# Weight subtractions moved on GpSimd and VectorE, and the gates computed ahead of the fill matmuls, in a Fourier mix followed by a mixture of experts

## The chip, the core and the metric

The kernel runs on one core of a Trainium2 chip. The core has TensorE (PE in the rows; PEld is its weight load), VectorE (DVE), ScalarE (ACT), GpSimd (POOL) and SyncE (SP, which here only issues DMAs). The metric is the time on the device in microseconds. Before the change the median of three runs was 593.81 us (592.75 to 595.03).

## The reference

The input x has 8 batches of 2496 tokens with 256 features. A Fourier transform along the tokens, a complex 256x256 product, a soft threshold and the inverse transform give 19968 rows; then each row is sent to one of 8 experts, and each expert computes only the 80 rows with the largest gate.

```python
X = np.fft.rfft(x, axis=1)
Yr = Xr @ w_r - Xi @ w_i + b_r
Yi = Xr @ w_i + Xi @ w_r + b_i
Yr = np.sign(Yr) * np.maximum(np.abs(Yr) - lam, 0.0)      # Yi too
y = np.fft.irfft(Yr + 1j * Yi, n=2496, axis=1)
...
logits = x @ w_gate                                      # x is y as (19968, 256)
expert_idx = np.argmax(logits, axis=1)
probs = softmax(logits); gate_w = probs[arange(N), expert_idx]
for e in range(8):
    tok_idx = the capacity=80 rows of expert e with the largest gate_w
    h = np.maximum(x[tok_idx] @ w1[e], 0.0)
    out[tok_idx] = gate_w[tok_idx, None] * (h @ w2[e])
```

## The kernel before

Both transforms are products with small tables, cut into stages: stageA and stageB are the forward transform (39 x 64 points), stageC the complex product with the soft threshold, stageT a transform over three classes on DVE, stageD a transposition back with the gate columns beside it, stageHB the last inverse step whose result goes to DRAM (`hd`). A loop over 16 steps (8 batches, two halves each) runs these stages interleaved. Values are split into a 16-bit high part and the remainder, so most products are three matmuls. Beside this, the 8 experts' weights are loaded in pieces of 128x1024, and each piece is split the same way: ACT copies the high part (L837, L840, L843) and a subtraction writes the low part, on POOL (L849) or, for the five pieces in the list `WV`, on DVE (L846). The pieces of experts 0 to 5 and part of 7 go to POOL; DVE has the four pieces of expert 6, numbered (k, i) with k = 0 for the first matrix and k = 1 for the second, and one of expert 7.

The last step of the loop (`if end`, L1500) is the second half of batch 7. Its stageC results (L441 matmuls, L450 on ACT, L456 and L458 on DVE) go to stageG1 (L676 matmuls), which computes the gate scores of this half directly. stageG0 and stageE1c complete the scores, `back` (L750) transposes them, stageE2 (L758 to L780) makes softmax gates, level1 and the rounds of level2 (L946 to L952) find each expert's best, and `pick` merges two lists (L1020 to L1027) and writes `posA`, the rows to gather (L1271). The function `stageT` (L503 to L508) and its copies (L516, L517) of the half before run on DVE at the beginning of this last step; `junk` (L1516) is a copy of one element on POOL that waits for them and that holds what is behind it on POOL.

From `posA` on POOL issues indirect DMAs: `tok` (row numbers), `hx` (the pieces of a row, two gathers for each group of 128 rows) and `wv` (their coefficients); `position` sums the pieces, `columnsY` transposes the sums into `xT`, `ffn1` (L1230, L1232, L1234) and `ffn2` (L1246, L1247) are the two products of an expert, and `give` scatters the rows into the output. `busy` (L1195) issues matmuls whose result is not used, to keep TensorE's clock up while the gathers run: 16 in front of the gate matmuls, 22 behind them. `rows` (L1274, L1276) turns the chosen gates into a column for each gathered row, with the help of `flat` (L1002, L1007), which spreads the 8 lists over a diagonal by multiplying with an identity and sums over TensorE. `flags` (L1034 to L1043) checks whether the quick selection may have missed a row.

The order of the instructions on each engine is set by a scheduler that goes by its own estimate of times. Three things steer it: `tc.high_priority()`, `tc.issue_after(i)` (not ahead of instruction i; `behind` is the same with a name), and `pin`, which keeps the written order.

## Time and profile before

| | before |
|---|---|
| median of 3 runs | 593.81 us |
| profiled execution, its own time | 594.43 us |
| its span | 592.6 us |
| PE busy | 531.8 us (90%) |
| DVE busy | 393.4 us (66%) |
| POOL busy | 379.3 us (64%) |
| ACT busy | 324.8 us (55%) |

The span is the time between the first and the last instruction of the profiled execution; what lies around it is 594.43 - 592.6 = 1.8 us. A row of a timeline has the start in us from the span's beginning, the time that the instructions take together, the engine, the line of the kernel, the operation, what is written and read with its size, and how many there are; in square brackets is how long the engine stood idle before it, and what it then waited for.

### The profile page before, as it was taken

To read this page: it belongs to the slowest core of one execution; us is meant where nothing else is said; L and a number is where in the kernel's file an instruction comes from. 1 tells how busy PE (TensorE), PEld (TensorE's weight loads), DVE (VectorE), ACT (ScalarE), POOL (GpSimd) and SP (SyncE) were. 2 spreads that over 40 slices of the span, in tenths; PEclk is the share of its full clock that TensorE was granted. 3 is DMA by queue.
4 is the path that set the end of the run, shared out by engine and by line. 5 is a ranking of instruction groups with operands and counts; after the bars stand their busy time and mean duration, and the time that the engine had idled before them with its cause. 6 is when DMAs were issued, how large, how long until landed. Compare 5 with 4: busy or idle time off the path is not lost.

```text
span 592.6 us, 12886 instructions
## 1 busy us (share of the span) xinstructions
PE 531.8 (90%) x5037; PEld 387.8 (65%) x5037; DVE 393.4 (66%) x738; ACT 324.8 (55%) x466; POOL 379.3 (64%) x301
## 2 busy tenths in 40 slices
PE   7869999999999999999999999896999598879683
PEld 2356576668677776877686777665767485448583
DVE  4423555666766667666777866768999847957550
ACT  2324868575756756575666566655646325623461
POOL 4104887686857777786778675688843634867571
PEclk9969999999999999999999999998999757996898
DMA  6887898987989789888979887999827766568810
GB/s 205 263 234 212 306 213 278 268 277 227 270 254 316 196 248 279 263 242 254 289 221 263 249 244 175 309 270 282 237 69 207 198 212 196 134 223 293 292 56 24
DMA packets 97225, 137.02 MB, mean 231 GB/s; under 512 B 26601, under 2 KB 77809, under 8 KB 95403
## 3 DMA queue, kind: packets, MB, share of 16 engines
q1 hardware_dynamic: 91115, 118.10, 69.3%
q0 software_dynamic: 2624, 11.45, 5.5%
q10 hardware_dynamic: 3418, 6.58, 3.4%
q8 instruction: 41, 0.67, 0.5%
q14 instruction: 27, 0.21, 0.1%
HBM read 70.82 MB, written 65.29 MB: 230 GB/s over the span
## 4 chain that ended last, share of the span: by engine, by line
PE 39%; DVE 14%; issue 14%; POOL 14%; DMA 12%; ACT 5%; SPq 1%; POOLq 0%; ACTq 0%; DVEq 0%
PE ps L441 20%; PE ps L311 5%; POOL pair L849 4%; PE ps L607 4%; DMA wt<-in_moe_w 4%; DVE R L470 2%; DMA xt<-in_x 2%; DMA hx<-hd,tok 2%; POOL R L473 2%; ACT tp L465 2%; PE ps L382 1%; PE ps L544 1%; PE ps L383 1%; PE ps L384 1%; PE ps L545 1%
## 5 line engine op out<-in xcount | busy, mean ns | idle before, releaser
L441 PE MATMUL ps<-XT,WM 128*128 128x288 f16 (+4 forms) x1536 | 217.0, 298 | 9.3 <-DVE R L470 3.8
L441 PEld LDWEIGHTS <-WM 128*128 128x128 f16 x1536 | 149.2, 98 | 66.9 <-issue 9.1
L470 DVE SCALAR_TENSOR_TENSOR R<-ps,thr,tp 128x674 f32<-128x674 f32 (+1 forms) x56 | 48.6, 867 | 76.4 <-ACT tp L465 72.7
L488 POOL TENSOR_TENSOR YT<-R,YT 128x1408 f16<-128x1408 f32 (+1 forms) x28 | 73.5, 2624 | 31.9 <-ACT YT L487 28.5
L465 ACT ACTIVATE tp<-ps,thr 128x674 f32<-128x674 f32 (+1 forms) x56 | 43.5, 777 | 79.1 <-PE ps L441 77.2
L473 POOL TENSOR_TENSOR R<-R,sgs 128x576 f32<-128x576 f32 x28 | 36.5, 1302 | 74.3 <-DVE R L470 74.3
L297 POOL TENSOR_TENSOR xs<-xt,xs 117x1024 f16<-117x1024 f32 (+1 forms) x39 | 76.2, 1956 | 9.9 <-ACT xs L296 9.8
L382 PE MATMUL ps<-t2s,z 128*128 128x128 f16 x320 | 59.3, 225 | 9.0 <-DMA z<-zs 7.7
L388 DVE TENSOR_TENSOR XT<-ps,XT 128x640 f16<-128x640 f32 (+2 forms) x64 | 51.7, 814 | 18.9 <-ACT XT L387 18.3
L333 DVE TENSOR_TENSOR zs<-ps,zs 128x1024 f16<-128x1024 f32 (+1 forms) x45 | 51.1, 1135 | 18.7 <-ACT zs L332 18.4
L383 PE MATMUL ps<-t2s,z 128*128 128x128 f16 x320 | 59.2, 224 | 0.0
L384 PE MATMUL ps<-t2s,z 128*128 128x128 f16 x320 | 59.2, 224 | 0.0
L387 ACT ACTIVATE XT<-ps 128x640 f16<-128x640 f32 (+2 forms) x64 | 44.4, 700 | 25.1 <-PE ps L384 22.7
L311 PE MATMUL ps<-xs,t1s 117*128 117x512 f16 x213 | 52.5, 379 | 1.0 <-POOL xs L297 0.8
L607 PE MATMUL ps<-YO,vqs 128*128 128x512 f16 (+1 forms) x252 | 48.6, 333 | 1.9 <-DVE hs L614 1.9
L332 ACT ACTIVATE zs<-ps 128x1024 f16<-128x1024 f32 (+1 forms) x45 | 42.9, 954 | 12.5 <-PE ps L311 6.3
L556 DVE TENSOR_TENSOR YO<-ps,YO 128x768 f16<-128x768 f32 (+1 forms) x50 | 45.3, 906 | 6.0 <-ACT YO L555 6.0
L487 ACT ACTIVATE YT<-R 128x1408 f16<-128x1408 f32 (+1 forms) x28 | 35.5, 1267 | 20.7 <-POOL R L484 20.7
L544 PE MATMUL ps<-wgi,YT 128*128 128x144 f16 (+1 forms) x302 | 43.9, 231 | 1.6 <-DVE R L470 1.3
L545 PE MATMUL ps<-wgi,YT 128*128 128x136 f16 (+1 forms) x302 | 43.2, 227 | 0.0
L555 ACT ACTIVATE YO<-ps 128x768 f16<-128x768 f32 (+1 forms) x50 | 38.5, 776 | 3.1 <-PE ps L545 1.4
L607 PEld LDWEIGHTS <-vqs 128*128 128x128 f16 x252 | 24.5, 99 | 23.8 <-issue 3.3
(317 smaller groups left out, 997.1 us busy)
## 6 DMA issues: line engine op xcount, KB each, us to landing
out<-zero SPq DMA_DIRECT2D x48, 384.0 KB
hd<-hs SPq DMA_DIRECT2D x94, 192.0 KB
z<-zs SPq DMA_DIRECT2D x35, 512.0 KB
xt<-in_x SPq DMA_DIRECT2D x41, 312.0 KB
z<-z SPq DMA_DIRECT2D x14, 528.0 KB
z<-z SPq DMA_DIRECT2D x14, 432.0 KB
wt<-in_moe_w ACTq DMA_DIRECT2D x10, 512.0 KB
pair<-in_moe_w SPq DMA_DIRECT2D x10, 512.0 KB
```

Source lines behind the costliest of these rows:

```text
L297: nc.gpsimd.tensor_tensor(xs[:, 1, :ng], xt[:, j0:j0 + ng], xs[:, 0, :ng], op=ALU.subtract)
L311: nc.tensor.matmul(pt[:, 512 * j:512 * j + 512], t1s[:, t], xs[:, h, 2 * j:2 * j + 2], start=(i == 0), stop=(i == 2))
L333: evD.append(nc.vector.tensor_tensor(zs[:, :ng, 1, :], pv[:, :ng], zs[:, :ng, 0, :], op=ALU.subtract))
L382: nc.tensor.matmul(o, zz(0), t2s[:, cl, 0, :], start=True, stop=False)
L383: nc.tensor.matmul(o, zz(0), t2s[:, cl, 1, :], start=False, stop=False)
L384: nc.tensor.matmul(o, zz(1), t2s[:, cl, 0, :], start=False, stop=True)
L388: nc.vector.tensor_tensor(ov(1), pv, ov(0), op=ALU.subtract)
L441: nc.tensor.matmul(pt[:, o:o + e - a], WM[:, dh, m, wh, 128 * eh:128 * eh + 128], XT[:, dh, xh, c, a:e], start=(i == 0), stop=(i == len(te ...
L465: acts.append(nc.scalar.activation(fv(t), pv, AF.Relu, bias=thr[:, eh, ri, 0:1]))
L470: nc.vector.scalar_tensor_tensor(fv(Rf), pv, thr[:, eh, ri, 1:2], fv(t), op0=ALU.add, op1=ALU.min)
L488: nc.gpsimd.tensor_tensor(yv(1), rv, yv(0), op=ALU.subtract)
L607: nc.tensor.matmul(o, tab[:, v], yo(h), start=(i == 0), stop=(i == 2))
```

## The change

Six edits. In the last step's first block, two subtractions (expert 3's first matrix) are held back in a list, and `junk` is issued first; they and the next two (expert 2's second matrix) are issued behind it. The last two copies and subtractions of that block are issued behind stageD's copy (`dev`) and not behind `acts`. The comparison L1021 goes from `merge` into `flags`. `rows` and `flags` are called in `pick`, with 6 fill matmuls ahead of them, and their small tiles lie in pools that are open by then; the later fill is 32. `flat` can take the identity from PSUM, into which it is copied first. The DVE subtractions of expert 6's second matrix (k = 1) are held back in `dheld` and issued in `experts`, behind `rv` of expert 0 (L1234).

```diff
--- before.py
+++ after.py
...
@@ -799,6 +801,7 @@
     dev, late, dvs = [], [], []
     LW = 7
     wdma = nc.scalar.dma_start
+    hold, held = [], []
     WV = [(6, 0, 0), (6, 0, 1)] + [(6, 1, 0), (6, 1, 1)] + [(7, 1, 1)]
 
     def prepW(e, pool, name):
@@ -842,11 +845,18 @@
                 with tc.issue_after((exps[-2], exps[-2], d2s[0], exps[-1])[2 * k + i].ins) if after else ExitStack():
                     nc.scalar.activation(wh[:, c:c + 1024], wt, AF.Copy)
             if (e, k, i) in WV:
-                with behind(("A", 'xv', (3, 4)[k])) if e == 7 and after else tc.issue_after((ffs if after and e == 6 and k + i else sels)[-1].ins):
-                    nc.vector.tensor_tensor(wl[:, c:c + 1024], wt, wh[:, c:c + 1024], op=ALU.subtract)
+                sub = lambda: nc.vector.tensor_tensor(wl[:, c:c + 1024], wt, wh[:, c:c + 1024], op=ALU.subtract)
+                if e == 6 and k and after:
+                    dheld.append(sub)
+                else:
+                    with behind(("A", 'xv', (3, 4)[k])) if e == 7 and after else tc.issue_after((ffs if after else sels)[-1].ins):
+                        sub()
             else:
-              with tc.issue_after(sums[-1].ins) if sums and e > 4 else ExitStack():
-                nc.gpsimd.tensor_tensor(wl[:, c:c + 1024], wt, wh[:, c:c + 1024], op=ALU.subtract)
+
+                def sub():
+                    with tc.issue_after(sums[-1].ins) if sums and e > 4 else ExitStack():
+                        nc.gpsimd.tensor_tensor(wl[:, c:c + 1024], wt, wh[:, c:c + 1024], op=ALU.subtract)
+                held.append(sub) if hold else sub()
         return [(e, lambda k=k, i=i: step(k, i), lambda k=k, i=i: load(k, i)) for k in range(2) for i in range(2)]
 
     def weight(e, k):
@@ -995,13 +1005,17 @@
 
     hevs = []
 
-    def flat(v, n, dt, late=None, px=None):
+    def flat(v, n, dt, late=None, px=None, eye=None):
 
         px = (sp.tile([8, 8 * CAP], dt, name="pxw") if px is None else px)[:, :8 * n].rearrange("p (e r) -> p e r", e=8)
+        pt = psum()
         with tc.issue_after(late[-1].ins) if late else ExitStack():
-            nc.vector.tensor_tensor(px, v.unsqueeze(1).to_broadcast([8, 8, n]), (eye8 if dt == F16 else ident)[:8, :8].unsqueeze(2).to_broadcast([8, 8, n]), op=ALU.mult)
+            i8 = (eye8 if dt == F16 else ident)[:8, :8]
+            if eye:
+                nc.vector.tensor_copy(pt[:8, 512:520], i8)
+                i8 = pt[:8, 512:520]
+            nc.vector.tensor_tensor(px, v.unsqueeze(1).to_broadcast([8, 8, n]), i8.unsqueeze(2).to_broadcast([8, 8, n]), op=ALU.mult)
         px = px.rearrange("p e r -> p (e r)")
-        pt = psum()
         m = n // 16
         for g in range(m):
             flats.append(nc.tensor.matmul(pt[:, g:g + 1], px[:, 128 * g:128 * g + 128], ones8h if dt == F16 else ones8, start=True, stop=True))
@@ -1018,7 +1032,6 @@
         fl = const.tile([128, 2, 8], F32, name="fl", tag="tk1")[:8, 0, :2]
         g, dp = room[:, :NEW], room[:, NEW:2 * NEW]
         nc.vector.tensor_scalar(fl[:, 0:1], v[:, k:k + 1], GATE_MIN, None, op0=ALU.max)
-        nc.vector.tensor_tensor(fl[:, 0:1], nv[:, NEW - 1:NEW], fl[:, 0:1], op=ALU.is_ge)
         rv, rp = nv[:, ::-1], np_[:, ::-1]
         nc.vector.tensor_tensor(g, rv, v[:, k:], op=ALU.is_gt)
         nc.vector.tensor_tensor(dp, rp, p[:, k:], op=ALU.subtract)
@@ -1029,18 +1042,20 @@
 
     def flags(bg, nw, fl):
         v, m, nm = bg[0], bg[2], nw[2]
-        th = sp.tile([8, 1], F32, name="th")
+        th = const.tile([128, 2, 8], F32, name="th", tag="tk3")[:8, 0, 0:1]
         with tc.issue_after(sels[-1].ins):
             nc.vector.tensor_reduce(out=th, in_=v, op=ALU.min, axis=AX.X)
         nc.vector.tensor_scalar(th, th, GATE_MIN, None, op0=ALU.max)
         with tc.issue_after(sels[-1].ins):
             nc.vector.tensor_tensor(m, m, nm, op=ALU.max)
+            nc.vector.tensor_tensor(fl[:, 0:1], nw[0][:, NEW - 1:NEW], fl[:, 0:1], op=ALU.is_ge)
         nc.vector.tensor_tensor(fl[:, 1:2], m, th, op=ALU.is_ge)
         pt = psum()
         fls.append(nc.tensor.matmul(pt[0:1, 0:2], ones8, fl, start=True, stop=True))
-        ff = sp.tile([1, 1], F32, name="ff")
+        ff = const.tile([128, 2, 8], F32, name="ff", tag="tk4")[:1, 0, 0:1]
         nc.vector.tensor_reduce(out=ff, in_=pt[0:1, 0:2], op=ALU.add, axis=AX.X)
-        ffs.append(nc.vector.tensor_copy(flag, ff))
+        with tc.issue_after(idms[-1].ins):
+            ffs.append(nc.vector.tensor_copy(flag, ff))
 
     NG = E * CAP // 128
 
@@ -1195,7 +1210,7 @@
             warms.append(nc.tensor.matmul(pt, w[:, 0:128], w[:, 0:512], start=True, stop=True))
 
     warms = []
-    BUSY = (16, 22)
+    BUSY = (6, 32)
 
     def columnsY(nm, g, y, xT, pt):
         if isinstance(y, tuple):
@@ -1271,8 +1286,9 @@
         sels.append(nc.vector.tensor_tensor(posA, pr, dl, op=ALU.add))
 
     def rows(nm, v, S):
-        nc.vector.tensor_scalar(gateA, flat(v, CAP, F32, sels), 1.0 / XS, None, op0=ALU.mult)
-        idm = sp.tile([128, NG], F32, name="idm" + nm)
+        A = nm == "A"
+        nc.vector.tensor_scalar(gateA, flat(v, CAP, F32, sels if A else None, px=spare()[:8] if A else None, eye=A), 1.0 / XS, None, op0=ALU.mult)
+        idm = const.tile([128, 2, 8], F32, name="idm", tag="tk5")[:, 0, :NG]
         idms.append(nc.vector.tensor_scalar(idm, gateA, GATE_MIN / XS, BIG, op0=ALU.is_lt, op1=ALU.mult))
 
         def rest():
@@ -1342,6 +1358,9 @@
         feedY(S)
         feedY(S)
         first(0)
+        with behind((S["nm"], "rv", 0)):
+            while dheld:
+                dheld.pop(0)()
         for e in range(E):
             h = hps.pop(e)
             if e:
@@ -1501,8 +1520,10 @@
             doC(0, 0)
             for k in range(4):
                 wq[k][2]()
+            hold.append(1)
             with tc.issue_after(acts[-1].ins):
                 doW(2)
+            hold.clear()
             with tc.issue_after(hbs[-1].ins):
                 while zq:
                     zfill()
@@ -1513,15 +1534,19 @@
             stageG1(b, RR[0], 0)
             with tc.high_priority():
                 stageG1(b, RR[1], 1)
-            pin(nc.gpsimd.tensor_copy(junk, prev[2][0:1, 1, 1, 0, 0, 0:1]))
-            with tc.issue_after(mids[-1].ins):
-                doW(2)
-            with tc.issue_after(acts[-1].ins):
-                doW(2)
+            jk = nc.gpsimd.tensor_copy(junk, prev[2][0:1, 1, 1, 0, 0, 0:1])
+            pin(jk)
+            with tc.issue_after(jk.ins):
+                while held:
+                    held.pop(0)()
+                with tc.issue_after(mids[-1].ins):
+                    doW(2)
             with tc.issue_after(cops[-1].ins):
                 doD()
             with tc.high_priority():
                 back = stageE1c(b, stageG0(b, prev[2]))
+            with tc.issue_after(dev[-1].ins):
+                doW(2)
             p = pend.pop()
             sc6 = stageE2(*p)
             doHB()
@@ -1671,11 +1696,16 @@
         pb_ = places("b", bg[1], CAP, 0.0)
         fl = merge((bg[0], pb_, bg[2]), (nw[0], places("n", nw[1], NEW, 512.0), nw[2]))
         choose(bg[0], pb_)
-        return fl
+        pt = psum()
+        for _ in range(BUSY[0]):
+            nc.tensor.matmul(pt[:, 0:512], pairs[0, 0][0][:, 0:128], pairs[0, 0][0][:, 0:512], start=True, stop=True)
+        rows("A", bg[0], S0)
+        flags(bg, nw, fl)
 
     with tc.issue_after(hops[-1].ins):
         doHB()
-    fl = pick()
+    S0 = {}
+    pick()
     flush()
     stacks[0].close()
     eks.close()
@@ -1697,11 +1727,9 @@
         pct = ctx.enter_context(tc.tile_pool(name="pct", bufs=1, space=PSUM, reuse_waits="tile"))
         pyp = ctx.enter_context(tc.tile_pool(name="pyp", bufs=1, space=PSUM, reuse_waits="tile"))
         pf = ctx.enter_context(tc.tile_pool(name="pf", bufs=4, space=PSUM, reuse_waits="tile"))
-        busy(BUSY[0], pairs[0, 0][0])
         sA = begin("A", NG, posA, cid[0:R2])
-        with tc.issue_after(warms[-1].ins):
-            rows("A", bg[0], sA)
-        flags(bg, nw, fl)
+        S0.update(ct=sA["ct"])
+        sA.update(rest=S0["rest"])
     doW(len(wq) - 4)
     with tc.issue_after(fls[-1].ins), tc.high_priority():
         busy(BUSY[1], pairs[0, 0][0])
```

The list `gps` is only written. The rows below are the engines' instruction orders; line numbers are those of the version that they belong to.

On POOL, in the last step of the loop, before the change (L458 and L517 belong to the stages, L849 is a weight subtraction, `pair_6064` holds expert 3, `pair2b` expert 2's second matrix):

```order
L458 TENSOR_TENSOR R<-R,sgs 128x9x64
L517 TENSOR_TENSOR YT_5755<-R,YT_5755 128x1408
L849 TENSOR_TENSOR pair_6064<-wt,pair_6064 128x1024 x2
L849 TENSOR_TENSOR pair2b<-st,pair2b 128x1024 x2
L1516 COPY junk<-YT_5755 1x1
L849 TENSOR_TENSOR pair_6064<-wt,pair_6064 128x1024 x2
```

and after it (L460, L519, L858 and L1537 are the same instructions' new lines):

```order
L460 TENSOR_TENSOR R<-R,sgs 128x9x64
L519 TENSOR_TENSOR YT_5755<-R,YT_5755 128x1408
L1537 COPY junk<-YT_5755 1x1
L858 TENSOR_TENSOR pair_6064<-wt,pair_6064 128x1024 x2
L858 TENSOR_TENSOR pair2b<-st,pair2b 128x1024 x2
L858 TENSOR_TENSOR pair_6064<-wt,pair_6064 128x1024 x2
```

Four subtractions stood ahead of the copy; all six now stand behind it.

On ACT a little later, before (L843 are weight copies, L666 and L555 belong to stageG0 and stageD, L771 is the exponential of batch 6):

```order
L450 ACTIVATE tp_144<-ps,thr 128x576
L843 ACTIVATE pair_6064<-wt 128x1024 x2
L666 ACTIVATE gp<-ps 128x88
L555 ACTIVATE YO_6071<-ps 128x2x256
L771 ACTIVATE gex<-ps 78x256
```

and after (L452, L846, L668, L557 and L773):

```order
L452 ACTIVATE tp_144<-ps,thr 128x576
L668 ACTIVATE gp<-ps 128x88
L557 ACTIVATE YO_6071<-ps 128x2x256
L846 ACTIVATE pair_6064<-wt 128x1024 x2
L773 ACTIVATE gex<-ps 78x256
```

The two copies went from ahead of stageG0's copy to directly ahead of the exponential.

On DVE behind `posA`, before (L846 are subtractions of expert 6, L1145 is the first work on gathered rows):

```order
L1271 TENSOR_TENSOR posA<-ps,dl 128x5
L1037 TENSOR_TENSOR t2b<-t2b,gh 8x1
L846 TENSOR_TENSOR pair_6811<-pair_6451,pair_6811 128x1024
L1002 TENSOR_TENSOR pxw<-t0b,ident 8x640
L1034 TENSOR_REDUCE th<-t0b 8x1
...
L1043 CAST flag<-ff 1x1
L846 TENSOR_TENSOR pair_6811<-pair_6451,pair_6811 128x1024 x3
L1145 TENSOR_TENSOR wt<-ident,wv 128x128
```

and after (L1015 is the copy of the identity, L1051 the moved comparison, L848 the subtractions):

```order
L1286 TENSOR_TENSOR posA<-ps,dl 128x5
L1015 COPY ps<-ident 8x8
L1047 TENSOR_REDUCE th<-t0b 8x1
L1050 TENSOR_TENSOR t2b<-t2b,gh 8x1
L1051 TENSOR_TENSOR fl<-gh,fl 8x1
L1017 TENSOR_TENSOR Gs<-t0b,ps 8x640
...
L1058 CAST flag<-ff 1x1
L848 TENSOR_TENSOR pair_6802<-pair_6451,pair_6802 128x1024 x2
L1160 TENSOR_TENSOR wt<-ident,wv 128x128
```

One subtraction left the place between `posA` and the gates, one left the place behind the flag; both now stand behind the second `L1249` (L1234 before) of expert 0, ahead of `xT` of group 1.

## Rows read from the trace of the kernel before

**Rows 1.** The page, part 1: an engine's busy time, share and instructions.

```profile
PE 531.8 (90%) x5037; PEld 387.8 (65%) x5037; DVE 393.4 (66%) x738; ACT 324.8 (55%) x466; POOL 379.3 (64%) x301
```

**Rows 2.** Windows: length; PE, PEld, DVE, ACT, POOL busy; granted clock, DMA share, GB/s.

```profile
466.00:468.00 2.00, 0.00 (x0) 0.00 (x0) 1.08 (x4) 1.33 (x2) 0.23 (x1) 0.88 0.06 19
...
486.00:488.00 2.00, 2.00 (x11) 0.99 (x9) 2.00 (x8) 0.43 (x1) 2.00 (x2) 0.50 0.04 8
```

**Rows 3.** Timeline of PE.

```profile
455.65 8.99 PE L441 MATMUL ps<-XT,WM 128*128 128x320 f16 x72
471.97 7.88 PE L676 MATMUL ps<-wgm,R 128*128 128x40 f32 x36 [7.33 <-DVE R L458]
...
532.65 1.22 PE L1209 MATMUL ps<-wt,hx 128*128 128x128 f32 x4 [2.81 <-DVE wt L1145]
```

**Rows 4.** Timeline of POOL in the last step.

```profile
456.64 4.79 POOL L849 TENSOR_TENSOR pair<-wt,pair 128x1024 bf16<-128x1024 f32 x2 [4.13 <-ACT pair L843]
461.40 4.83 POOL L849 TENSOR_TENSOR pair2b<-st,pair2b 128x1024 bf16<-128x1024 f32 x2
...
485.56 4.21 POOL L849 TENSOR_TENSOR pair<-pair,pair 128x1024 bf16<-128x1024 f32 x2 [9.05 <-PE ps L736]
```

**Rows 5.** Tile hs from 440 us: smallest, median, largest ns, first and last start.

```profile
L505 DVE TENSOR_TENSOR R<-R,hs x2: 548/1462/2375, 445.0 to 457.1; 128x384 f32<-128x384 f32 x2
L506 DVE SCALAR_TENSOR_TENSOR R<-hs,R x2: 559/1155/1751, 445.6 to 460.1; 128x384 f32<-128x384 f32 x2
L507 DVE SCALAR_TENSOR_TENSOR R<-hs,R x2: 558/1460/2362, 446.2 to 461.9; 128x384 f32<-128x384 f32 x2
L508 DVE SCALAR_TENSOR_TENSOR R<-hs,R x2: 548/1454/2360, 447.6 to 464.3; 128x384 f32<-128x384 f32 x2
```

**Rows 6.** Timeline of DVE in the last step.

```profile
457.07 2.38 DVE L505 TENSOR_TENSOR R<-R,hs 128x384 f32<-128x384 f32 x1
459.37 0.80 DVE L456 SCALAR_TENSOR_TENSOR R<-ps,thr,tp 128x576 f32<-128x576 f32 x1
...
468.08 1.62 DVE L517 TENSOR_TENSOR YT<-R,YT 128x1408 f16<-128x1408 f32 x1 [0.97 <-ACT YT L516]
```

**Rows 7.** Timeline of ACT in the last step.

```profile
466.67 1.38 ACT L516 ACTIVATE YT<-R 128x1408 f16<-128x1408 f32 x1 [7.11 <-DVE R L508]
...
473.14 1.06 ACT L843 ACTIVATE pair<-wt 128x1024 f16<-128x1024 f32 x1 [0.92 <-DMA wt<-in_moe_w]
...
481.91 0.60 ACT L555 ACTIVATE YO<-ps 128x512 f16<-128x512 f32 x1
484.16 0.38 ACT L771 ACTIVATE gex<-ps 78x256 f32<-78x256 f32 x1 [1.65 <-DVE ps L770]
```

**Rows 8.** Timeline of SP's queue: the second weight load into the staging halves.

```profile
468.71 0.67 SPq L822 DMA_DIRECT2D wt<-in_moe_w  x1
```

**Rows 9.** Timeline of DVE and of POOL at the end of the selection.

```profile
515.27 1.04 DVE L1021 TENSOR_TENSOR fl<-gh,fl 8x1 f32<-8x1 f32 x1
...
512.08 4.23 POOL L849 TENSOR_TENSOR pair<-pair,pair 128x1024 bf16<-128x1024 f32 x2
```

**Rows 10.** Timeline of POOL and of DVE behind posA.

```profile
519.81 1.84 POOL L1094 DMA_INDIRECT tok<-cid,posA  x1 [3.50 <-DMA hd<-hs]
521.96 0.96 POOL L1094 DMA_INDIRECT tok<-cid,posA  x1 [0.31 <-issue]
525.74 1.88 POOL L1094 DMA_INDIRECT hx<-hd,tok  x1 [2.83 <-issue]
...
519.50 1.21 DVE L846 TENSOR_TENSOR pair<-pair,pair 128x1024 bf16<-128x1024 f32 x1
...
524.45 3.50 DVE L846 TENSOR_TENSOR pair<-pair,pair 128x1024 bf16<-128x1024 f32 x3
```

**Rows 11.** Timeline of DVE, and the chain that ended last (start, us, what).

```profile
545.04 0.42 DVE L1217 TENSOR_TENSOR xT<-ps,xT 128x256 f16<-128x256 f32 x1 [1.52 <-ACT xT L1216]
...
547.75 8.17 DMA hx<-hd,tok
```

More of the change, by code (lines that the diff above doesn't have):

```diff
@@ L415, in fourier_mix_then_moe @@
     mids = []
+    gps = []
+    dheld = []
     d2s = []
@@ L645, in stageE1a @@
         gp = ek.tile([128, 2, 20, 8], F16, name="gp", bufs=2)
-        nc.scalar.activation(gp[:, 0], G, AF.Copy)
+        gps.append(nc.scalar.activation(gp[:, 0], G, AF.Copy))
         nc.vector.tensor_tensor(gp[:, 1], G, gp[:, 0], op=ALU.subtract)
@@ L665, in stageG0 @@
         nc.vector.tensor_reduce(out=G, in_=pt[:, 0:176].rearrange("p (c h e) -> p c e h", h=2, e=8), op=ALU.add, axis=AX.X)
-        nc.scalar.activation(gp[:, 0], G, AF.Copy)
+        gps.append(nc.scalar.activation(gp[:, 0], G, AF.Copy))
         nc.vector.tensor_tensor(gp[:, 1], G, gp[:, 0], op=ALU.subtract)
```

## Prediction

> **What bounds the kernel now.** I read the page first: no engine is full over the whole span (PE 90%), so the time has to be read by stretches [rows 1]. A table of 2 us windows then shows where PE stands still near the end: from 466 to 468 PE does nothing, its clock falls there, and it is still at half speed (0.50, the 1.2 GHz level) at 486 [rows 2]. From there on the kernel is a chain of short steps (gate scores of the last batch, selection, gathers, experts) in which every delay is passed on to the end.
>
> The timelines of the three engines say why PE stood still. PE ends its last L441 matmul at 455.65 + 8.99 = 464.64 and begins L676 (stageG1) at 471.97, waiting 7.33 us for DVE's L458 [rows 3]. DVE was late because POOL ran four weight subtractions (L849) from 456.64 to 466.23 [rows 4]. Inside that time DVE's L505 to L508 took 2.375, 1.751, 2.362 and 2.360 us, where the same four took 0.548, 0.559, 0.558 and 0.548 us ten microseconds earlier: the smallest and the largest of each line's two instances stand in its row [rows 5]. All four read two operands from SBUF. L456 at 459.37, which reads PSUM and one SBUF tile, took 0.80 us in the same stretch [rows 6]. So a DVE instruction with two SBUF inputs lasts until POOL's running instruction ends, and one with a PSUM input does not care.
>
> **The change part by part, against the profiled execution (594.43 us with a span of 592.6; the median of the three runs shown is 593.81, 0.6 lower).**
>
> 1. *The subtractions go behind the junk copy.* Four of POOL's six subtractions of this stretch now stand behind the one-element copy that waits for DVE's L517; the other two stood there already. While L505 to L508 run, POOL is idle. They give back 8.85 - 2.21 = 6.6 us. I walk it through: DVE 457.07 + 0.55 + 0.80 + 0.56 + 0.56 + 0.55 = 460.1; ACT's L516 (1.38) to 461.5; L517 (1.62) to 463.1, where it ended at 469.70 [rows 6, 7]. From there to L676 nothing is changed: 471.97 - 6.6 = 465.4. PE's last L441 ends at 464.64, before that, so PE does not bind first. Value -6.6; the bounds are -7.3 (the whole gap on PE) and -4 (one blocked instruction of 2.4 comes back).
>
> 2. *The clock in stageG1.* Before, the clock was at half 2.9 us after the last L441 (a mean of 0.88 over 466 to 468 is a fall near 467.5) and did not rise although PE is shown busy for all of 486 to 488 and from 471.97 on [rows 2, 3]. Now the gap is under 1 us. What PE then does is 36 matmuls of 40 columns (7.88 us at half speed), and no row shows them at full speed. If the clock still falls where it fell relative to the last L441 (near 467.5), some 2 us of stageG1 run at full speed and save about 1.5. If it never falls, 3.9 go in stageG1 and about 2.5 in the matmuls behind it. Bounds 0 and -6.4; I take -1.5, because PE was busy for long in this very work without getting the clock back.
> The Trainium skill (TensorE: Matmul & The Clock Gate, Part 1) says that the clock is throttled by default and that activity releases it, an idle stretch bringing the throttle back. Taken as it stands it would keep the clock up here and give -6.4 in place of -1.5; the busy stretch at 0.50 in this trace speaks against counting this work as such activity. It is the first rival below.
>
> 3. *The last two ACT copies (L843, the second at 473.14) go behind L555 and so directly ahead of the exponential L771* [rows 7]. L771 began at 484.16, 1.65 us after L555's end at 482.51. Two copies of 1.06 fill that and push it by about 0.5. Most of it lies beside PE's matmuls for the same DVE step. Value +0.2. Their data come over SP into the two staging halves, which POOL's first two subtractions now free at about 465.5 and 467.7 (463.3 and twice about 2.2) instead of 459 and 461.4. The second transfer took from its issue at 468.71 [rows 8] to the copy that waited for it at 473.14, 4.4 us; so it should land near 472. It is wanted when the second copy starts, 482.51 + 1.06 - 8.1 (points 1 and 2) = 475.5. Cover: 3.5 us; past it each microsecond counts fully.
>
> 4. *The flag comparison L1021 leaves the selection.* It took 1.04 us because POOL's last subtraction held it until 512.08 + 4.23 = 516.31 [rows 9]. L1023 behind it has two SBUF inputs as well and will wait for the same subtraction. Value 0, bounds -0.9 and +2 (POOL's row ending later against DVE's).
>
> 5. *Gates and flags ahead of the fill, identity in PSUM.* Behind posA DVE ran a weight subtraction (1.21) and L1002; the first gather ran beside them and took 1.84 us; the first hx gather ran beside three more and took 1.88. The gather between took 0.96 [rows 10]. Now L1002 reads the identity from PSUM, and only two subtractions are left there, which end near 525.4 on the old time scale, against a gather due at 525.74 - 0.9 = 524.8. So the first delay (0.9) goes and about 0.6 of the second. All later gathers are issued behind these on one queue. Value -1.5, bounds 0 and -1.85. The gate matmuls move from after 16 fill matmuls to after 6, and the later fill grows from 22 to 32; PE waits for gathered data there (idle for 2.81 us before 532.65 [rows 3]), which hides both, and takes more fill with it: 0, with 0 and +0.5 as bounds.
> The Trainium skill (SBUF — State Buffer, section "Who interferes with whom") infers that a tensor_tensor takes only the read side of the port that DVE and GpSimd share, while writing a gather's descriptors needs the write side. By that this part would give 0 and the sum would be -7.4 (586.4, inside the forecast's own range); the two long gathers beside two-input DVE work say otherwise here.
>
> 6. *The other two DVE subtractions go behind the first expert's second L1234.* Two of 1.2 us start at about 543.5, where DVE was idle for 1.52 until L1217 [rows 11]. L1217 moves by about 0.9. PE has expert 0's second product in hand until about 546.3 and hides it. POOL issues gathers at that time, which the subtractions can hold up; each later issue reaches the end, since the chain there is a gather landing (8.17 us) [rows 11]. Value +0.5, bounds 0 and +1.8.
>
> Everything else (SP sending the gate tables ahead of two weight loads, tiles moved to other pools) costs no instruction on the path: 0.
>
> Sum: -6.6 - 1.5 + 0.2 + 0 - 1.5 + 0.5 = -8.9, so 585.5 for the profiled execution and 584.9 from the median.
>
> **Rivals.**
>
> *The clock holds through stageG1.* For it: PE's gap shrinks from 7.33 to under 1 us. Against it: the busy stretch at 0.50. Term 2 is -6.4: 593.8 - 13.8 = 580.0.
>
> *POOL's backlog takes part of it back.* All of POOL's work now starts at 463 instead of 456.6, and the selection starts earlier. If POOL's last subtraction ends 4 to 5 us later relative to the selection, L1023 to L1027 and L1002, all with two SBUF inputs, wait one after another. For it: POOL was busy right up to 516.3 and L1021 already waited for it. Against it: POOL was idle 9.05 us before 485.56 [rows 4]. Price +4.5: 589.4.
>
> *No change.* The transfers bind: the chain comes earlier but the gathers or the weight loads land when they did. Against it: the share is 0.06 in 466 to 468 and 0.04 in 486 to 488 [rows 2], and the gathers are issued by the chain itself. 592 to 594.
>
> *Slower: the exponential waits for a weight load.* The chain of point 3: held subtractions free the staging halves later, SP sends the loads behind the gate tables, which must wait for one another, and ACT, which works in order, holds L771 and all behind it. It decides from the moment the second load lands past 475.5; slower than before it is when that is past 475.5 + 8.9 = 484.4, which at a landing time of 4.4 needs SP to be held until 480. At 489 it gives 593.8 + 4.6 = 598.4.
>
> **How the numbers follow.** My forecast (terms within their bounds, 582 to 588): 62%. Clock holds: 16%. Backlog: 11%. No change: 6%. Slower: 5%. The predicted time is 584.9. The range goes from 579.5 (the clock holds) to 589.6 (the backlog) and leaves out the last two cases and the far ends of the bounds, some 15%. A difference under 0.5% (3 us) could not be told from none; faster by more is the first three cases, 0.89; within it 0.06; slower 0.05.
>
> **What the new profile would show.** Right: L505 to L508 (their new line numbers are two higher) at 0.55 us each; POOL's subtractions starting near 463; stageG1 on PE starting near 465.4 and less than 1 us after the last L441-type matmul; its 36 matmuls in 4 to 8 us, which with the granted clock settles term 2; posA about 8 us earlier; the first tok and hx gathers at about 0.95 and under 1.5 us. Wrong: stageG1 starting after 468; ACT idle before the exponential until a DMA; two-input DVE instructions of 2 us ahead of posA; gathers still of 1.8 us; the stretch from posA to the end longer than before (592.6 - 519.8 = 72.8 us from the first tok gather).

## The result, and the profile after

The changed kernel takes 587.31 us (median of four runs, 585.12 to 588.99) where the kernel before takes 594.35 beside it: ratio 0.9883, 95% interval 0.9844 to 0.9923, or 7.0 us less (4.6 to 9.3). Run again in a later series, as a2, it gave 0.9901 (0.9864 to 0.9937). The forecast was 584.9 with 579.5 to 589.6. The profiled execution of the changed kernel took 588.99 us with a span of 587.2, the longest of the four.

The timeline of PE in the changed kernel (start, us busy, line, tiles, and the idle time ahead with its releaser in brackets); L443 and L678 are the L441 and L676 of [rows 3]:

```profile
454.65 8.99 PE L443 MATMUL ps<-XT,WM 128*128 128x320 f16 x72
464.34 6.15 PE L678 MATMUL ps<-wgm,R 128*128 128x40 f32 x36 [0.70 <-DVE R L460]
...
533.16 0.29 PE L1245 MATMUL pf<-xT,pair 128*128 128x80 f16 x2 [4.17 <-issue]
533.62 2.29 PE L1245 MATMUL pf<-xT,pair 128*128 128x80 f16 x32 [0.17 <-issue]
536.21 0.22 PE L1245 MATMUL pf<-xT,pair 128*128 128x80 f16 x1 [0.30 <-issue]
536.95 0.22 PE L1245 MATMUL pf<-xT,pair 128*128 128x80 f16 x1 [0.51 <-issue]
```

The wait of 7.33 us is 0.70, and the 36 matmuls take 6.15 in place of 7.88. The last four rows are the start of a pause (to 540.55) in which PE, with single or few matmuls, waits for nothing that the profile shows; no such thing stands in the profile of before, and it comes back below. The 4.17 us ahead of it are the wait for ScalarE's copy L1231, which itself stood 2.98 us for nothing on record:

```profile
532.72 0.38 ACT L1231 ACTIVATE xT<-ps 128x256 f16<-128x256 f32 x1 [2.98 <-issue]
```

The windows say when the clock fell (columns as in [rows 2]):

```profile
464.00:466.00 2.00, 1.66 (x15) 1.69 (x16) 1.71 (x3) 0.42 (x1) 2.00 (x2) 1.00 0.31 21
466.00:468.00 2.00, 2.00 (x13) 2.00 (x12) 0.36 (x2) 0.00 (x0) 2.00 (x2) 0.56 0.16 45
```

The mean of 0.56 is a fall near 466.2 to the 1.2 GHz level, although PE had worked through but for the 0.70. The four instructions of VectorE that were held up (tile hs; smallest, median and largest ns of the two instances of a line, as [rows 5]):

```profile
L507 DVE TENSOR_TENSOR R<-R,hs x2: 548/553/558, 444.0 to 456.1; 128x384 f32<-128x384 f32 x2
L508 DVE SCALAR_TENSOR_TENSOR R<-hs,R x2: 548/554/559, 444.6 to 457.3; 128x384 f32<-128x384 f32 x2
L509 DVE SCALAR_TENSOR_TENSOR R<-hs,R x2: 558/558/559, 445.2 to 457.9; 128x384 f32<-128x384 f32 x2
L510 DVE SCALAR_TENSOR_TENSOR R<-hs,R x2: 550/554/559, 446.6 to 458.4; 128x384 f32<-128x384 f32 x2
```

Both instances now take 0.55. The other engines in the timeline of the changed kernel, to be laid beside [rows 4, 7, 9 and 10]:

```profile
462.14 0.18 POOL L1537 COPY junk<-YT 1x1 f16<-1x1 f16 x1 [10.63 <-DVE YT L519]
462.40 4.22 POOL L858 TENSOR_TENSOR pair<-wt,pair 128x1024 bf16<-128x1024 f32 x2
...
472.55 0.60 ACT L557 ACTIVATE YO<-ps 128x512 f16<-128x512 f32 x1
473.05 1.99 ACT L846 ACTIVATE pair<-wt 128x1024 f16<-128x1024 f32 x2
474.94 0.37 ACT L773 ACTIVATE gex<-ps 78x256 f32<-78x256 f32 x1
...
505.86 1.75 DVE L1036 TENSOR_TENSOR Gs<-gh,t0b 8x48 f32<-8x48 f32 x1
...
503.34 4.21 POOL L858 TENSOR_TENSOR pair<-pair,pair 128x1024 bf16<-128x1024 f32 x2
...
510.06 1.16 SPq L823 DMA_DIRECT2D pair<-in_moe_w  x2
...
510.98 1.06 POOL L1109 DMA_INDIRECT tok<-cid,posA  x1 [3.44 <-DMA hd<-hs]
512.35 0.96 POOL L1109 DMA_INDIRECT tok<-cid,posA  x1 [0.30 <-DMA hd<-YO]
516.97 1.17 POOL L1109 DMA_INDIRECT hx<-hd,tok  x1 [3.67 <-DMA tok<-cid,posA]
```

The subtractions begin at 462.40, the two copies stand directly ahead of the exponential without a wait for their loads, and L1036 waits for GpSimd's last subtraction (its end is 503.34 + 4.21 = 507.55). The first gathers take 1.06 and 1.17 as forecast. But from the first tok gather to the first hx gather it is 516.97 - 510.98 = 5.99 us, where before it was 525.74 - 519.81 = 5.93 [rows 10]: VectorE's gain at the first issue came out as a longer wait for the landing. The gain at the hx gather (1.17 for 1.88) remains: the wv gather behind it starts 7.47 us behind the first tok gather, where it was 8.12. The rows of before and of the changed kernel:

```profile
527.93 0.95 POOL L1094 DMA_INDIRECT wv<-in_vt,tok  x1 [0.30 <-issue]
...
518.45 0.95 POOL L1109 DMA_INDIRECT wv<-in_vt,tok  x1 [0.30 <-issue]
```

Where the 5.4 us between the two profiled spans stand: the exponential comes 9.2 us earlier (1.0 of that was there at 456, before anything changed), posA 8.8, the first work on gathered rows 8.35; the stretch from there to the end is 63.24 us against 60.29, and that is the pause. One sign that the prediction named against itself came true by it: from the first tok gather to the end it is 587.2 - 510.98 = 76.2 us, where before it was 72.8. In a2, without the pause, it is 579.1 - 507.92 = 71.2.

One table for all profiles. "Gap" is PE's wait ahead of stageG1, "36" its matmuls; the other columns are lengths of stretches, cut at the end of the last L441-type matmul, the first exponential of the last step (L771 of before), the end of posA, and VectorE's first work on gathered rows (L1145 of before). "Clock" is TensorE's mean granted clock from that exponential to posA, with 1 for 2.4 GHz and 0.50 for 1.2 GHz. "Order" is ScalarE's order around the third group's copy, explained at the f kernels; the last column, whether the pause is there.

| kernel | gap | 36 | to exponential | to posA | clock | to first work | to end | order | pause |
|---|---|---|---|---|---|---|---|---|---|
| before | 7.33 | 7.88 | 19.52 | 35.37 | 0.85 | 12.78 | 60.29 | old | no |
| f0 | 7.33 | 7.87 | 19.51 | 36.56 | 0.78 | 12.04 | 64.27 | new | yes |
| e2 | 7.33 | 7.88 | 19.51 | 32.60 | 0.91 | 12.44 | 56.56 | new | no |
| f2 | 7.33 | 7.87 | 19.51 | 35.26 | 0.85 | 11.98 | 64.01 | new | yes |
| changed | 0.70 | 6.15 | 11.30 | 35.76 | 0.83 | 13.26 | 63.24 | old | yes |
| a2 (changed) | 0.69 | 5.13 | 10.72 | 33.12 | 0.95 | 11.97 | 59.49 | old | no |
| e1 | 0.69 | 4.18 | 10.50 | 34.36 | 0.87 | 13.10 | 60.54 | old | no |
| f1 | 0.70 | 5.73 | 10.87 | 36.27 | 0.78 | 11.46 | 63.01 | new | yes |
| f3 | 0.70 | 4.96 | 10.72 | 34.25 | 0.90 | 13.67 | 60.76 | new | in part |
| f3b | 0.70 | 6.11 | 11.26 | 35.76 | 0.83 | 11.94 | 55.68 | new | no |
| e4 | 0.69 | 6.04 | 11.19 | 35.76 | 0.83 | 11.92 | 56.63 | new | no |
| e4b | 0.69 | 5.15 | 10.54 | 33.33 | 0.95 | 12.14 | 56.64 | new | no |
| g1 | 0.69 | 4.18 | 11.17 | 35.33 | 0.84 | 9.42 | 58.08 | new | no |
| g2 | 0.69 | 4.18 | 10.35 | 33.60 | 0.77 | 13.70 | 55.76 | new | no |

The stretch to posA goes with the clock in it: 33.1 to 33.3 us at 0.95, 34.3 to 34.4 at 0.87 and 0.90, 35.3 to 35.8 at 0.83 to 0.85, 36.3 to 36.6 at 0.78. Only e2 and g2 lie below that line. The same program stands at two places of it (changed and a2, e4 and e4b), so some 2.5 us between two executions go with this clock and not with a change of the kernel.

### The profile page after: what moved, and what is told of

Its sections match the earlier page's. It is cut to its first block, busy times and chain, and to the rows that moved or that the text cites. A ratio compares the mean times of both kernels' runs of the same rounds, so it can differ in the third digit from the quotient of the medians.

```text
span 587.2 us, 12890 instructions
## 1 busy us (share of the span) xinstructions
PE 532.3 (91%) x5037; PEld 387.2 (66%) x5037; DVE 388.1 (66%) x739; ACT 324.6 (55%) x466; POOL 376.7 (64%) x301
## 4 chain that ended last, share of the span: by engine, by line
PE 43%; DVE 15%; DMA 13%; issue 10%; POOL 9%; ACT 6%; SPq 2%; POOLq 0%; ACTq 0%; DVEq 0%
PE ps L443 21%; PE ps L311 5%; DMA wt<-in_moe_w 4%; PE ps L609 4%; DMA xt<-in_x 2%; DVE R L472 2%; POOL R L475 2%; ACT tp L467 2%; PE ps L546 2%; DMA out<-zero 2%; PE ps L547 2%; PE ps L382 1%; PE ps L383 1%; PE ps L384 1%; PE pf L1245 1%
## 5 line engine op out<-in xcount | busy, mean ns | idle before, releaser
L443 PE MATMUL ps<-XT,WM 128*128 128x288 f16 (+4 forms) x1536 | 215.7, 297 | 7.5 <-DVE Gs L561 2.1
L443 PEld LDWEIGHTS <-WM 128*128 128x128 f16 x1536 | 148.7, 98 | 64.2 <-issue 7.5
L297 POOL TENSOR_TENSOR xs<-xt,xs 117x1024 f16<-117x1024 f32 (+1 forms) x39 | 76.2, 1955 | 9.9 <-ACT xs L296 9.8
L557 ACT ACTIVATE YO<-ps 128x768 f16<-128x768 f32 (+1 forms) x50 | 38.4, 774 | 3.1 <-PE ps L547 1.1
```

The source lines that it names most:

```text
L297: nc.gpsimd.tensor_tensor(xs[:, 1, :ng], xt[:, j0:j0 + ng], xs[:, 0, :ng], op=ALU.subtract)
L443: nc.tensor.matmul(pt[:, o:o + e - a], WM[:, dh, m, wh, 128 * eh:128 * eh + 128], XT[:, dh, xh, c, a:e], start=(i == 0), stop=(i == len(te ...
```

## The experiments

**Which part carries it: e1, e2, a2.** e1 is the kernel before with the first part alone; e2 is the changed kernel with that part undone.

```diff
-              with tc.issue_after(sums[-1].ins) if sums and e > 4 else ExitStack():
-                nc.gpsimd.tensor_tensor(wl[:, c:c + 1024], wt, wh[:, c:c + 1024], op=ALU.subtract)
+                held.append(sub) if hold else sub()
...
-            pin(nc.gpsimd.tensor_copy(junk, prev[2][0:1, 1, 1, 0, 0, 0:1]))
+            jk = nc.gpsimd.tensor_copy(junk, prev[2][0:1, 1, 1, 0, 0, 0:1])
+            with tc.issue_after(jk.ins):
+                while held:
+                    held.pop(0)()
```

> The kernel before with the first part of the change alone: POOL's four subtractions held behind the one-element copy, and the last pair of weight steps behind the last D stage. Theory A (the forecast's steps 1 to 3 are the whole of this part): the last L441-type matmul and stageG1 follow each other within 1 us, stageG1 takes 6 to 6.5 us, and the time falls by 6.6 + 1.7 = 8.3 up to the selection, so about 586.1, with the first tok and hx gathers still at 1.8 us each. Rival B (the gain is undone behind the selection because the gathers or weight loads set the pace there): posA comes 8 us earlier and the time falls by no more than 4 us (590 or more). Rival C (the later parts carry a good part of the measured 7.0): 589 to 591 with the gathers at 1.8 us.

> The changed kernel with the first part undone: the subtractions stand ahead of the one-element copy again; gates, flags, identity in PSUM and the two late VectorE subtractions stay. Theory A: the 7.3 us gap on PE ahead of stageG1 is back and only the terms of steps 5 and 6 remain (-1.5 and +0.5), so about 593.3, which this measurement can't tell from before. Rival C: the later parts are worth 3 us or more by themselves: 591.3 or less. If the tail of the changed kernel holds a loss of its own of 2 to 3 us, as its profile showed between 529 and 540, then 595 to 596.

> The changed kernel once more, unchanged. Theory E (the pause of 3 to 4 us on ScalarE and TensorE at 529 to 540 in its profile is instruction fetch, held up by the gathers that fill the DMA engines, and depends on when the block is asked for): the pause is there again, at the same instructions, in most profiles, and the span from the first work on gathered rows to the end is 62 to 64 us. Rival F (chance in one execution): no such pause, 60 to 61 us from the first work to the end, and a time near 585.

Measured, on one chip: e1 584.63 us, ratio 0.9905 (0.9869 to 0.9941); e2 586.29, 0.9951 (0.9905 to 0.9996); a2 583.69, 0.9901 (0.9864 to 0.9937), with before at 590.61. The timeline of PE in e1:

```profile
464.80 4.18 PE L676 MATMUL ps<-wgm,R 128*128 128x40 f32 x36 [0.69 <-DVE R L458]
...
528.47 0.23 PE L1234 MATMUL pf<-xT,pair 128*128 128x80 f16 x2 [0.92 <-ACT xT L1220]
529.05 1.81 PE L1234 MATMUL pf<-xT,pair 128*128 128x80 f16 x46 [0.35 <-DVE xT L1221]
```

and in e2:

```profile
471.12 7.88 PE L678 MATMUL ps<-wgm,R 128*128 128x40 f32 x36 [7.33 <-DVE R L460]
```

The first part alone removes the gap, and the whole change is no faster than it. It came out smaller in time than theory A said (-6 for -8.3), with a shorter stageG1 (4.18 us for 6 to 6.5) and a first hx gather of 0.94 us for 1.8, and e2 faster than theory A said (-4.3 for -1), which spoke for rival C until the f kernels below. a2 has no pause (rival F for this execution); e1's first product runs through in 1.81 us where the changed kernel's takes from 533.16 to 540.55.

**ScalarE's order: the f kernels.** The table's column "to end" fell into groups that had nothing to do with the change: e2 and e4 had 56.6, a2 and e1 59.5 and 60.5. Between them ScalarE's order differs around one place. In a2's timeline of ACT:

```profile
542.35 0.91 ACT L1190 ACTIVATE hx<-hx,wv 128x256 f32<-128x256 f32 x2 [2.73 <-issue]
543.16 0.46 ACT L1185 ACTIVATE yp<-hx,wv 128x256 f32<-128x256 f32 x1
543.56 0.36 ACT L1231 ACTIVATE xT<-pt 128x256 f16<-128x256 f32 x1
```

Two scalings of the fourth group stand 2.73 us, and behind them stands the copy L1231 of the third group, whose input PE had ready at 541.2. What they wait for the profile does not name here. The kernel before has the same order, and there it is a gather (its L1175 waits 3.17 us for the 8.17 us landing of [rows 11]), so the order is no part of the change. The f kernels put the two behind that copy:

```diff
-                with behind((nm, *LATER[g][0])):
+                with behind((nm, "xa", 2) if g == 3 and r > 6 else (nm, *LATER[g][0])):
```

> The kernel before, with one thing altered on ScalarE alone: the two scalings of the fourth group's second gathered half (L1175, rows 7 and 8), which waited 3.17 us for their gather at 555.99 with the third group's copy L1216 behind them, are issued behind that copy. Theory H (ScalarE works in order, so the wait of these two is passed on to the third group and to the end): the wait is off the path, time before less 2 to 3 us, ratio 0.995 to 0.997. Rival G (the gathers' landing sets the end anyway, the order is worth nothing): ratio 1.000.

> The same ScalarE order, with the first part of the change (POOL's subtractions behind the one-element copy) and no other. Theory A (steps 1 and 2 of the forecast, -8.3 in stageG1's start and length, nothing of it given back): 7 to 8 us under f0_before_acts. If a part of it is given back behind the selection, as the first comparison of this part alone with before (0.9905, some 5.6 us) suggests: 5 to 6 us under it, and the stretch from posA to the end longer by 1 to 2 us than in f0.

> The same ScalarE order, with the other parts of the change (gates and flags ahead of the fill, identity in PSUM, two subtractions of VectorE late) and without the first. Theory A (step 5 -1.5, step 6 +0.5): 0.5 to 1.5 us under f0_before_acts. Rival C (these parts are worth 3 us or more by themselves, as the 4.3 us of the earlier run without the first part would say if its ScalarE order had no share in it): 3 to 4.5 us under f0.

> The changed kernel with the same ScalarE order. Theory H: the 2.73 us for which ScalarE waited in the changed kernel's second profile are gone and the time is 2 to 3 us under the changed kernel, ratio to before about 0.984. Theory A adds up: 8 to 9 us under f0_before_acts and 0.5 to 1.5 under f1_part1_acts. Rival G: no better than the changed kernel (0.988 to 0.990).

Measured, on one chip with before at 592.95: f0 592.63, 0.9996 (0.9966 to 1.0026); f1 584.13, 0.9851 (0.9811 to 0.9892); f2 593.60, 1.0006 (0.9977 to 1.0036); f3 586.01, 0.9870 (0.9831 to 0.9909). With one order and one chip in all four, the attribution of the first part is clear: it is worth 8.5 us without the others (f0 to f1) and 7.6 with them (f2 to f3). The others are worth nothing that can be measured (f0 to f2: +1.0, f1 to f3: +1.9, the intervals overlap), where theory A had them 0.5 to 1.5 us faster. Rival C fails here. Why e2 had gained stays open, and ScalarE's order alone does not explain it: f2 gives every engine the same instructions in the same order as e2, and it gained nothing (1.0006 for 0.9951). Theory H failed here: f0 is no faster than before, and f3 lies at rival G's end. All four profiles have the pause, f3 only in part: f1 and f2 show a series of single or few matmuls like the changed kernel, and f0 the longest. In f3 it is ScalarE that stands for nothing on record, 2.79 us ahead of its L1231, and TensorE's 3.91 us are the wait for that copy:

```profile
532.47 0.38 ACT L1231 ACTIVATE xT<-ps 128x256 f16<-128x256 f32 x1 [2.79 <-issue]
```

The timeline of PE in f0:

```profile
538.56 2.12 PE L1230 MATMUL pf<-xT,pair 128*128 128x80 f16 x34 [0.35 <-issue]
541.12 0.24 PE L1230 MATMUL pf<-xT,pair 128*128 128x80 f16 x1 [0.44 <-issue]
542.53 0.23 PE L1230 MATMUL pf<-xT,pair 128*128 128x80 f16 x1 [1.17 <-issue]
```

The last 12 of these 48 matmuls end at 548.60, most of them single and 0.7 us apart, and by the time the third group is due its gathers have landed: the wait that the new order would avoid was gone already. So f3 was run again:

> The changed kernel with ScalarE's two scalings behind the third group's copy and the identity still in PSUM, once more. Its first run had TensorE's pause at the first expert's product in its profile (585.0 us span, 0.987); the kernel with the identity in SBUF and the same ScalarE order had none in two runs (0.983, 0.978). Theory K (the order is worth 3 us where the pause is absent, the identity's place nothing): 0.978 to 0.983 if the profile shows no pause, with 56 to 57 us from the first work on gathered rows to the end; 0.986 to 0.988 and 60 us or more if it does. Rival P (the identity's place is what made the difference): 0.987 to 0.990 with no pause in the profile.

Measured, on another chip: 580.19 us, 0.9821 (0.9791 to 0.9851), no series of single matmuls, 55.68 us from the first work to the end. The timeline of ACT in f3b at the same place:

```profile
543.52 0.48 ACT L1185 ACTIVATE yp<-hx,wv 128x256 f32<-128x256 f32 x1 [0.33 <-DVE y L1198]
544.02 0.38 ACT L1231 ACTIVATE xT<-pt 128x256 f16<-128x256 f32 x1
544.30 0.90 ACT L1190 ACTIVATE hx<-hx,wv 128x256 f32<-128x256 f32 x2
```

The copy passes and the scalings no longer wait. The run fits theory K, by which the order is worth 3 us where the pause is absent and nothing where it is there (its 55.68 us lie just under the 56 to 57 expected). The profiles without any pause read the same way: 59.5 to 60.5 us to the end with the old order (three), 55.7 to 58.1 with the new (six). On one chip e4, in the next part, is 3.4 us under a2 (580.25 for 583.69); the two differ in the identity's place too. In the times of f0 the gain does not show: its fastest of twelve executions took 589.88 us, and the fastest of before beside it 589.15. Either all twelve had the pause, or the order is worth less than the profiles say; only one of the twelve has its profile here, so this stays open.

**The first gather and what it waits for: e4, e4b, g1.** e4 gives the gates' product its identity from SBUF again.

```diff
-        nc.vector.tensor_scalar(gateA, flat(v, CAP, F32, sels if A else None, px=spare()[:8] if A else None, eye=A), 1.0 / XS, None, op0=ALU.mult)
+        nc.vector.tensor_scalar(gateA, flat(v, CAP, F32, sels if A else None, px=spare()[:8] if A else None, eye=None), 1.0 / XS, None, op0=ALU.mult)
```

> The changed kernel with the gates' identity read from SBUF in place of PSUM, so that the 8x640 product beside the first tok gather has two SBUF inputs. Theory A (a two-input SBUF instruction of VectorE holds up the gather that GpSimd writes): the product of 0.80 us lengthens the first tok gather from 1.06 to 1.5 to 1.9 us and the chain by 0.4 to 0.8, 587.8 to 588.1. Rival D (the gather was long for another reason, such as being the first on its queue): 1.0 to 1.1 us, no change in time. If the pause of ScalarE and TensorE between 529 and 540 belongs to this instruction stream it is there again in this profile; if it is chance it is gone.

> The changed kernel with the gates' identity read from SBUF, once more, as the base of the next two and to see whether its 0.9834 of before stands on another chip and in more rounds. Theory K (its ScalarE order lets the third group's copy pass the two scalings that wait for a gather, worth 3 us when the pause of TensorE at the first expert's product is absent): 0.983 to 0.985 where the profile shows no pause, 0.987 where it does. Rival F (chance): 0.988, as the changed kernel.

Measured: 580.25 us, 0.9834 (0.9799 to 0.9868), and on another chip 578.40, 0.9778 (0.9731 to 0.9824), with the new ScalarE order in both (the scheduler chose it here unasked). The second is better than theory K and rival F expected. The first gather takes 1.38 in both. Over all profiles its length goes strictly with what VectorE does beside it: 1.06 with the PSUM product (six profiles), 1.37 to 1.38 with the SBUF product (four), 1.83 to 1.88 with a subtraction and the SBUF product (four). Theory A is right about the gather and wrong about its worth: from its start to the first hx gather it is 5.7 to 7.2 us in the profiles with 1.83 to 1.88, and 5.6 to 6.7 in those with 1.06. g1 asks what sets that length, by leaving two loads out:

```diff
             if (k, i) in got:
                 return
+            if e == 6 and k and after:
+                got[k, i] = got[0, i]
+                return
```

> The same with two of expert 6's weight loads left out (1 MB; the second half of its second matrix is taken from the first matrix's staging tiles, so this kernel leaves out part of the weights). They are issued by SyncE 0.5 us ahead of the first tok gather. Theory J (these loads fill the DMA engines while the tok gather lands, and so swallow what the shorter first gather saves): the time from the first tok gather's start to the first hx gather falls from 6.1 to 4.0 to 4.6 us and the whole by 1.5 to 2 us. Rival L (the landing is latency of the indirect transfer itself): 5.7 to 6.2 us as before, the whole within 0.5 us.

Measured: 577.17 us, 0.9751 (0.9703 to 0.9798), beside e4b's 578.40. The timeline of POOL in g1:

```profile
509.99 1.37 POOL L1112 DMA_INDIRECT tok<-cid,posA  x1 [3.43 <-DMA hd<-hs]
511.66 0.96 POOL L1112 DMA_INDIRECT tok<-cid,posA  x1 [0.30 <-issue]
513.49 0.94 POOL L1112 DMA_INDIRECT hx<-hd,tok  x1 [0.87 <-issue]
```

The first hx gather comes 3.50 us behind the first tok gather, where e4b has 6.46 and e4 6.12. Theory J holds for this wait: the two weight loads of 512 KB that SyncE issues just ahead of the tok gather lengthen it by some 3 us, more than expected, and a shorter gather only waits longer. In time it is 1.2 us, less than the 1.5 to 2 expected and with overlapping executions (576.21 to 579.02 beside 578.04 to 579.53): the stretch to the end is 1.4 longer (58.08 against 56.64).

**The selection's wait: g2.** GpSimd's last subtraction ahead of the selection's end goes behind the second tok gather (with the new ScalarE order).

```diff
-                    with tc.issue_after(sums[-1].ins) if sums and e > 4 else ExitStack():
+                    with tc.issue_after(gis[1].ins if (e, k, i) == (5, 1, 1) else sums[-1].ins) if sums and e > 4 else ExitStack():
```

> The same as the first of these three, with GpSimd's last weight subtraction (expert 5) moved from ahead of the selection's end to behind the second tok gather, where GpSimd waits some 3.5 us for that gather to land; the load that waits for its buffer goes with it, and ScalarE's two scalings stand behind the third group's copy. Theory M (step 4: the comparison of the selection waits 1.75 us for that subtraction): L1036 takes 0.2 us, posA comes 1.5 us earlier and the whole is 1 to 1.5 us faster. Rival N (posA comes earlier, but VectorE's subtraction of expert 6 and GpSimd's now lie side by side, or the late load holds ScalarE): the first hx gather comes no earlier, the whole within 0.5 us or slower.

Measured: 578.53 us, 0.9781 (0.9733 to 0.9829), the same as e4b. The timeline of g2, DVE and POOL:

```profile
503.15 0.20 DVE L1036 TENSOR_TENSOR Gs<-gh,t0b 8x48 f32<-8x48 f32 x1
508.77 2.77 DVE L1292 TENSOR_SCALAR idm<-gateA 128x5 f32<-128x5 f32 x1
511.52 2.34 DVE L848 TENSOR_TENSOR pair<-pair,pair 128x1024 bf16<-128x1024 f32 x2
...
509.38 2.13 POOL L858 TENSOR_TENSOR pair<-pair,pair 128x1024 bf16<-128x1024 f32 x1
512.24 2.46 POOL L1109 DMA_INDIRECT hx<-hd,tok  x1 [0.73 <-POOL pair L858]
```

L1036 takes 0.20 as theory M says, and the stretch to posA is short for its clock (33.60 us at 0.77). But GpSimd's subtraction now holds VectorE's L1292 for 2.77 us, so VectorE's own subtractions slide under the first hx gather, which takes 2.46. The first hx gather does come earlier than in e4b (512.24 for 514.27), against rival N's words, but the first work on gathered rows comes 13.70 us behind posA for e4b's 12.14. In time it is rival N that holds, by the collision that it named.

## Why the prediction was right, point by point

1. *Subtractions behind the copy, -6.6.* Right to a tenth: 7.33 less 0.70 is 6.63, the same in all ten profiles that have this part, and 7.33 in all four that have not. No later term came near it. The f kernels show that the first part, which is steps 1 to 3, is the whole effect that can be measured.

2. *The clock in stageG1, -1.5.* -1.73 in the changed kernel, -2.7 as a mean over the ten (5.18 for 7.88). In three of them the 36 matmuls took 4.18, all at full speed; the clock then fell behind them. The value was set low by its own working: with the fall 2.9 us behind the last L441 and a gap of 0.7, some 2.1 us run at full speed, which by the prediction's halving saves 2.1 and not 1.5. It was also read off one execution, and over the fourteen profiles the clock falls 2.6 to 5.5 us behind the last L441-type matmul. The rival by which the clock holds came true for stageG1 alone in three profiles. Behind stageG1 the clock fell in all of them, but in a2 and e4b it came back early (0.95 as the mean to posA), and there the stretch is 2.0 to 2.3 us shorter than before, near the 2.5 that the rival had priced. The rule of the Trainium skill that the prediction weighed (TensorE: Matmul & The Clock Gate, Part 1) would have kept the clock up with a gap of 0.70; the 0.56 of the window above says that it did not here.

3. *Two copies ahead of the exponential, +0.2.* From L557's end at 473.15 to the exponential it is 1.79 us, where it was 1.65: +0.14. The second copy followed the first without a wait for its load, so the slower rival's condition was never near.

4. *The flag comparison, 0.* L1036 took 1.75 for L1021's 1.04: +0.7, inside the bounds, for the reason given there (the next instruction waits for the same subtraction). The 0.7 is chance: L1036 took 1.03 in a2, and L1021, in its old place, 1.91 in f0.

5. *Gates, flags and the identity, -1.5.* This step failed in its larger half. Both gathers shortened as said, but the prediction took the whole of it for a gain of the chain. What the chain waits for behind the first is the landing of the tok rows, and that is lengthened by the weight loads in flight (g1): 5.93 before and 5.99 after. Only the hx gather's gain was passed on to the gathers behind it: -0.65 (7.47 for 8.12, and 7.48 in a2). At the first work on gathered rows it does not stand out (13.26 and 11.97 for 12.78 behind posA), nor in the times (f0 to f2 and f1 to f3). The rule of the Trainium skill named there (SBUF — State Buffer, "Who interferes with whom") would have given 0, and the 1.06, 1.38 and 1.83 to 1.88 of the first gather contradict its reason.

6. *VectorE's late subtractions, +0.5.* They ran in a2 from 530.79 to 533.14, and its timelines of POOL and PE show what they held up:

```profile
530.85 1.98 POOL L1109 DMA_INDIRECT wv<-in_vt,tok  x1 [0.30 <-DVE hp L1249]
...
533.53 1.81 PE L1245 MATMUL pf<-xT,pair 128*128 128x80 f16 x46 [0.66 <-DVE xT L1232]
```

The wv gather issued beside them took 1.98 in place of 0.95 (e1, without them), so that the gathers behind it come a microsecond later, and PE waited 0.66 for L1232 behind them: +0.7 to +1.0.

The terms with their sizes in the profiles: -6.6 - 1.7 + 0.1 + 0.7 - 0.65 + 0.7 = -7.45. The runs say -7.0 (4.6 to 9.3 less), and a2 -5.8 (3.7 to 8.0 less). The prediction's -8.9 lies inside the first interval and outside the second, so by the medians it was some 2 to 3 us too good. Steps 4 and 5 account for 1.5 of that; the rest is not tied to a step. That the time fell inside the range owes most to step 1; where in the range it fell is also chance, since some 2.5 us between executions go with the clock alone. Of the rivals, no change and slower are out; the backlog was there in its small form of step 4 and not in the 4 to 5 us that it was priced at.

What the prediction did not see lies at and behind the first expert and is not the change's: the pause, which lengthened the changed kernel's profile by some 3 to 4 us (63.24 for a2's 59.49), and ScalarE's order, which by the profiles cost both kernels about as much where the pause was absent. With the order mended and no pause, the changed kernel gave 0.9821 (f3b) and its near versions 0.9834, 0.9778 (e4, e4b) and 0.9781 (g2), against 0.9883 and 0.9901 as it stands; these beat both kernels. Save for e4 with a2 they are comparisons across chips.

What holds TensorE and ScalarE in the pause stays open. It is there in four profiles, in part in f3 and absent in nine, for the same program both ways (the changed kernel and a2, f2 and e2, f3 and f3b), so no edit made it. The four profiles of f0 to f3, all from one chip, have it, wholly or in part, and none of the eight from the three other chips on record, so it may go with the chip or with the series as well as with chance; no run separates these. The paused profiles of the changed kernel, f0 and f2 are the longest executions of their series, so they are not typical of its median. In f0 the DMA engines were 0.92 to 1.01 busy from 542 to 548 while PE worked 0.23 to 0.34 of the time:

```profile
542.00:544.00 2.00, 0.51 (x3) 0.13 (x2) 0.00 (x0) 0.00 (x0) 1.39 (x3) 0.50 0.92 338
546.00:548.00 2.00, 0.45 (x2) 0.21 (x2) 0.00 (x0) 0.00 (x0) 0.00 (x0) 0.50 1.01 294
```

The Trainium skill (Runtime: NRT & Kernel Launch, "Instruction fetch mechanics") says that an engine's sequencer fetches its next block of instructions over a DMA queue of its own while it works; a fetch held up by the gathers would look like this, but no run here shows that it was. Two profiles speak against it: they list the DMA packets of the kind instruction, and none moved in the changed kernel from 529.42 to 541.46 us, nor in f2 from 539.27 to 551.53, while the pauses ended at 540.55 and 550.23. A block that came late would have come before they ended.

## What to carry to other kernels

When a two-input instruction of VectorE takes a multiple of its usual time, look at what GpSimd runs beside it and at the tile's smallest and largest duration: here that one reading gave the gain to a tenth. A shorter issue is worth little while the landing it leads to is set by other transfers in flight, so price the landing, not the issue. An in-order engine should not meet an instruction that waits for a gather ahead of one whose input is ready, and here such a gain showed only in profiles where nothing else was late. Before two executions are compared, lay their granted clocks side by side: here 2.5 us between executions of one program went with it.

## What the runs showed of the hardware

- A gather's issue on GpSimd takes 0.94 to 0.96 us alone and is stretched by VectorE's work on SBUF beside it: 1.38, 1.83 to 1.88, 1.98 and 2.46 by what ran there; with a PSUM operand in the product it was 1.06.
- Not only two-input instructions wait for GpSimd: in g2 the one-input TENSOR_SCALAR L1292 (128x5) took 2.77 us beside a subtraction, and 0.17 in e4b beside a gather alone.
- Two weight loads of 512 KB in flight lengthened the wait for a gather of row numbers from 3.50 to 6.46 us (g1, e4b; one profile each).
- The 36 matmuls of 40 columns take 4.18 us at the full clock and 7.88 at half; over fourteen profiles the clock falls 2.6 to 5.5 us behind the matmuls ahead of them (L441-type).
- The stretch from the exponential to posA takes 33.1 us at a mean granted clock of 0.95 and 35.8 at 0.83, in two executions of the same program (a2, the changed kernel).
- TensorE can stand for 7 us with single matmuls 0.7 us apart and no wait on record, while gathers fill the DMA engines.
